# A tuned attention and feed-forward kernel: its instruction order taken from a longer search, with refitted durations

## The chip, the cores and the metric

The kernel runs on one core of one Trainium2 chip. The metric is device time in microseconds (us). Before the change the median of the first three runs was 248.99 us (248.48 to 249.06). A difference of over 2% counts as faster or slower here.

The engines are TensorE (PE; its weight loads PEld), VectorE (DVE), ScalarE (ACT), GpSimd (POOL) and the queue engine SyncE (SP). L706 in a row means line 706 of that kernel; line numbers differ between kernels.

## The reference

```python
def _attn_ref(q, k, v, n_global, n_local):          # q, k, v: 4 x 8 x 768 x 64
    scores = scale * np.matmul(q, k.transpose(0, 1, 3, 2))
    ...                                             # keep: 8 global keys, or the last 96
    scores = np.where(keep, scores + bias, -1000000000.0)
    a = np.exp(scores - np.max(scores, axis=-1, keepdims=True))
    return np.matmul(a / (np.sum(a, axis=-1, keepdims=True) + 1e-09), v)

def _moe_ref(x, w_gate, w_val, w_out, rms_g):       # x: 3072 x 512, hidden width 1536
    xn = x / np.sqrt(np.mean(x * x, axis=-1, keepdims=True) + 1e-06) * rms_g
    g = xn @ w_gate
    return (g * (1.0 / (1.0 + np.exp(-g))) * (xn @ w_val)) @ w_out
```

This is shortened. Attention with a local band and a few global keys is followed by a gated feed-forward layer (FFN) on its output.

## The kernel before

The 3072 tokens are cut into 8 chunks of 384. Every operation is first entered in a list with an estimated duration, a due position, its dependencies and the buffers it takes and gives. A list scheduler then runs through this list with its own clock, and writes each instruction in the order in which it starts them. The search shifts the priorities of groups of operations at random and keeps a step if the planned end is no later. All of this happens when the kernel is built. The chip sees only the resulting order.

```python
    START = {"SP": 0.7, "ACT": 0.7, "POOL": 1.4}     # us until a transfer begins
...
    def search(self, tries, keys, spread):

        rnd, best, shift = random.Random(7), math.inf, {}
        groups = sorted({key for o in self.ops for key in keys(o)}, key=str)
        for k in range(tries):
            new = dict(shift)
            if k:
                part = rnd.choice((0.05, 0.2, 1.0))
                amp = rnd.choice(spread)
                for g in groups:
                    if rnd.random() < part:
                        new[g] = new.get(g, 0.0) + rnd.uniform(-amp, amp)
            for o in self.ops:
                o.shift = sum(new.get(g, 0.0) for g in keys(o))
            end = self.run(call=False)
            if end <= best:
                best, shift = end, new
        for o in self.ops:
            o.shift = sum(shift.get(g, 0.0) for g in keys(o))
        self.run()
...
    # run(): the planner's loop, cut
    t0 = min(cand)[0] + slack                        # of what could start now, the lowest rank
    _, _, t, o = min((r, n, t, o) for t, r, n, o in cand if t <= t0)
    ...
    if call:
        ins = o.fn(*o.args, *([] if o.only else [eng]))   # emit the instruction here
    ...
    return self.free["PE"]                           # the planned end: when TensorE is done
```

These are the operations that the argument touches: the gate behind which chunk 1's keys and queries are transferred, the PE transposes of the first chunks, the root of the norm, and the padding matmuls.

```python
    held = [seq_ops["raw", "k", HP - 2]]             # pair 2 of chunk 0's raw keys
    if c == 1:
        held = seq_ops["gate"] = [add("POOL", 0.15, base, gate, "k1", deps=held, take=[bb["k"]])]
    for x, n in enumerate("kq"):
        o = add("POOL", 1.0, base + x, load_heads, c, n, kb=2.35, packet=49, ...)
...
    o = add("PE", (0.42, 0.68, 0.5)[c], due, tr, c, p, name, ...)      # transposes of q and k
...
    sq = [add("DVE", 0.16, a, ssum, c, deps=sq)]
    r = add("POOL", 1.1 if c >= NX else 0.9, a + 2, rstd, c, deps=sq)
...
    pad = add("PE", 1.1, a + 3.9, idle, c, deps=norms, take=t)
...
    TRIES = 200
...
    plan.search(TRIES, keys, (1.0, 3.0, 8.0))
```

The softmax here doesn't subtract the row's maximum and nothing guards it: scores larger than these inputs give would overflow.

Of the kernel before, what the change touches and what calls it, by code (L numbers as in the profile page):

```python
# [39 lines left out]
class _Plan:  # L40
# [10 lines left out]
    SLOW = ("xn", "glob_v", "kg", "cast_v", "copy_vg")  # L51

    ORDERED = ("mask", "xn", "glob_v", "kg")
    START = {"SP": 0.7, "ACT": 0.7, "POOL": 1.4}

    OVERLAP = {"PE": 0.0, "ACT": 0.1, "DVE": 0.08, "POOL": 0.06, "SP": 0.0}
    LAG = {"PE": 0.2, "ACT": 0.1, "DVE": 0.1, "POOL": 0.12, "SP": 0.0}
# [14 lines left out]
    def add(self, eng, dur, due, fn, *args, deps=(), take=(), give=(), extra=0.0, kb=0.0,  # L72
            packet=20):




        o = _Op()
        o.eng, o.durs = (None, eng) if isinstance(eng, dict) else (eng, {eng: dur})
        o.due, o.fn, o.args = due, fn, args  # L80
        o.deps, o.take, o.give = [d for d in deps if d is not None], list(take), list(give)
        o.extra, o.kb, o.done, o.n, o.shift, o.only = extra, kb, None, len(self.ops), 0.0, o.eng
        o.packet = packet
        self.ops.append(o)
        return o
# [67 lines left out]
        q = self.queues.get(eng)  # L153
        return q[-1][3].done - 4.3 if q else t

    def search(self, tries, keys, spread):

        rnd, best, shift = random.Random(7), math.inf, {}
        groups = sorted({key for o in self.ops for key in keys(o)}, key=str)
        for k in range(tries):  # L160
            new = dict(shift)
            if k:
                part = rnd.choice((0.05, 0.2, 1.0))
                amp = rnd.choice(spread)
                for g in groups:
                    if rnd.random() < part:
                        new[g] = new.get(g, 0.0) + rnd.uniform(-amp, amp)
            for o in self.ops:
                o.shift = sum(new.get(g, 0.0) for g in keys(o))
            end = self.run(call=False)  # L170
            if end <= best:
                best, shift = end, new
        for o in self.ops:
            o.shift = sum(shift.get(g, 0.0) for g in keys(o))
        self.run()
# [86 lines left out]
def kernel(  # L262
# [42 lines left out]
    NX = 4  # L305
# [71 lines left out]
    ident = const.tile([128, 128], BF16, tag="ident")  # L377
# [344 lines left out]
    def gate(what):  # L722
# [8 lines left out]
        else:  # L731
# [5 lines left out]
    plan = _Plan(  # L737
        sizes=dict(m=5, sc=2, av=1, P0=4, P1=4, u=2, t=3, h=2, xT=2, xu=2, xn=2, ob=3, sq=4, sk=4,
                   sv=4, qb=2, kb=2, qT=2, kT=2, kG=2, ld=999),
        free=dict(PE=0.8, ACT=2.1, DVE=0.85, POOL=0.8, SP=0.8))  # L740
    add, buf = plan.add, plan.buf
# [28 lines left out]
    seq_ops, const_ops, xn_gate = {}, {}, []  # L770

    def early_part(c):

        b, half = divmod(c, 2)
        q_ops, k_ops, v_ops = {}, {}, {}
        qT_buf[c], kT_buf[c] = buf("qT", HP), buf("kT", (16, 4, 5)[c])
        ld, vs, gs = {}, [], []
        base = START + (-30, 10, 60)[c]
        gated = []

        def load_v():
            for i in range(HB):
                sb = buf("sv")
                if c == 2 and i == 0:
                    gated.append(add("POOL", 0.15, START, gate, "v2", deps=[w_ops["o", 2]], take=[sb]))
                ld["v", i] = add("SP", 0.5, base + 5 + i, load_block, c, "v", i, kb=1.17, packet=20,
                                 take=[] if c == 2 and i == 0 else [sb], deps=gated), sb

        bb = {n: buf(n + "b", HP) for n in "qk"}
        if c == 0:  # L790
            for p in range(HP):
                for n in "qk":
                    eng = "ACT" if (p, n) == (0, "k") else "SP"
                    sb = buf("s" + n)
                    o = add(eng, 0.5, base + p if p < 2 else base + 10 + p, load_pair, p, n, eng, kb=0.6, packet=39, take=[sb])
                    seq_ops["raw", n, p] = o
                    ld[n, p] = add({"DVE": 0.36, "ACT": 0.5, "POOL": 0.55}, 0.5, START + 8 * p - 1, cast_pair, p, n,
                                   deps=[o], take=[] if p else [bb[n]], give=[sb]), bb[n]
            load_v()
        else:  # L800
            held = [seq_ops["raw", "k", HP - 2]]
# [3 lines that stand above are left out]
                o = add("POOL", 1.0, base + x, load_heads, c, n, kb=2.35, packet=49,  # L805
                        take=[] if (c, n) == (1, "k") else [bb[n]], deps=held)
                seq_ops["heads", c, n] = o
                for p in range(HP):
                    ld[n, p] = o, bb[n]
            load_v()  # L810
        for key, (o, _) in ld.items():
            seq_ops["ld", c, key[0], key[1]] = o
        due = (START - 1.0, S1 - 2.0, S2 - 2.0)[c]
        for i in range(HB):
            o, sb = ld["v", i]
            if c == 0:
                e1, e2 = {"POOL": 0.63, "ACT": 0.6, "DVE": 0.43}, {"POOL": 0.63, "ACT": 0.6, "DVE": 0.3}
            else:
                e1, e2 = {"POOL": 0.63}, {"POOL": 0.63}
            vs.append(add(e1, 0, due, cast_v, c, i, deps=[o] + (xn_gate if c else []), give=[sb]))  # L820
            if 0 < HB * half + i < NB - 1:
                gs.append(add(e2, 0, due + 0.1, copy_vg, c, i, deps=vs[-1:]))
        lo, hi = max(HB * half, 1), min(HB * half + HB, NB - 1)
        old = [glob[c - 1]] if half else []
        glob[c] = add({"DVE": 0.41, "POOL": 1.25}, 0, due, glob_v, b, lo, hi, deps=gs + old)
        kg_due = due
        for p in range(HP):
            v_ops[p] = vs + [glob[c]] + old
            due = (START + 8 * p, S1 + 2 * p, S2 + 4 * p)[c]
            for name, ops in (("q", q_ops), ("k", k_ops)):  # L830
                if c and p % 2:
                    ops[c, p] = ops[c, p - 1]
                    continue
                t = buf("m")
                o = add("PE", (0.42, 0.68, 0.5)[c], due, tr, c, p, name, deps=[ld[name, p][0], const_ops["ident"]] + hold.get(c, []),
                        take=[t], give=[ld[name, p][1]] * (2 if c else 1))
                tk = [] if p else [(qT_buf if name == "q" else kT_buf)[c]]
                ops[c, p] = [add({"ACT": 0.78} if c == 1 else {"ACT": 0.78, "DVE": 0.95} if c else {"ACT": 0.5, "DVE": 0.5}, 0, due + 1, cp, c, p, name, deps=[o],
                                 give=[t], take=tk)]
        if c >= NK:  # L840
            kG_buf[c] = buf("kG", HP if half else HP + 1 + HP)
            o = add({"DVE": 0.45 if half else 0.56, "POOL": 0.9 if half else 1.05}, 0, kg_due + 2, kg, c,
                    deps=[x for p in range(HP) for x in k_ops[c, p]], take=[kG_buf[c]],
                    give=[kT_buf[c]] + ([kT_buf[0]] if half else []))
            for p in range(HP):
                kg_ops[c, p] = o
        return q_ops, k_ops, v_ops
# [51 lines left out]
    def attention(c, q_ops, k_ops, v_ops):  # L899
# [4 lines left out]
        norms = []  # L904
        old_k.update(k_ops)
        for p in range(HP):
            yield
            a = a0 + 4 * p if b else START + 8 * p if c == 0 else S1 + 2 * p
# [18 lines left out]
            for d in range(2) if c == 0 else ():  # L927
# [3 lines left out]
                deps = q_ops[c, p] + k_ops[c, p]  # L931
# [23 lines left out]
        else:  # L955
# [3 lines left out]
                           ssq, c, i, part, deps=norms[:HP - 1] if part == 1 else norms,  # L959
                           give=[xu_b] if part == 1 else []) for i in range(HB)]  # L960
            sq = [add("DVE", 0.16, a, ssum, c, deps=sq)]
        r = add("POOL", 1.1 if c >= NX else 0.9, a + 2, rstd, c, deps=sq)
        xnb, xtb = buf("xn", 1 if c >= NX else HB), buf("xT", FC)
        x = [add({"DVE": 0.61} if c >= NX else {"DVE": 0.36} if c == 0 else {"DVE": 0.36, "ACT": 0.62}, 0.61, a + 3, xn, c, i, deps=[r], give=[xu_b],
                 take=[xnb] if i == 0 else []) for i in range(HB)]
# [2 lines left out]
        if c < NX:  # L968
            t = [buf("m", 2), buf("m", 2)]
            if c == 0:  # L970
                pad = add("PE", 1.1, a + 3.9, idle, c, deps=norms, take=t)
            o = [add("PE", 0.23, a + 4, xtr, c, i, deps=[x[i]] + ([pad] if c == 0 else []), take=[] if i or c == 0 else t, give=[xnb])
                 for i in range(HB)]
            for i in range(1, HB):
                o[i].deps.append(o[i - 1])
            done = [add({"DVE": 0.42, "ACT": 0.58}, 0, a + 5, xev, c, cc, deps=o, give=[t[cc // 2]],
                        take=[] if cc else [xtb]) for cc in range(CC)]
        else:
            done = [add("SP", 2.4, a + 4, dma_xt, c, deps=x, give=[xnb], take=[xtb], kb=1.8, packet=22)]
# [27 lines left out]
                at += 0.5  # L1007

    XNP = 1.15
    TRIES = 200  # L1010
    START, S1, S2, LEAD, DRAIN = -200.0, -22.0, -10.0, 26.0, 20.0
    def constants():
        S = START
# [49 lines left out]
                          reason="order at the shared port")  # L1063

    plan.follow = follow
    plan.search(TRIES, keys, (1.0, 3.0, 8.0))

# [1 line left out]
_INS = ['q', 'k', 'v', 'n_global', 'n_local', 'moe_w_gate', 'moe_w_val', 'moe_w_out', 'moe_rms_g']  # L1069
# [31 lines left out]
```

## Time and profile before

| | before |
|---|---|
| median of the first three runs | 248.99 us |
| span of the profiled run | 247.2 us |
| first matmul | 6.36 us |
| first FFN matmul | 25.23 us |
| end of the last matmul | 244.06 us |

The page of the kernel before gives the chain that ended last by line, as shares of the span, and then the costliest groups of instructions: line, engine, operation, tiles, shape, count, then busy us and mean ns, then idle time of the engine before them.

```profile
PE gps L675 24%; PE vps L682 23%; PE ops L706 22%; PE sc L536 4%; DMA kb<-in_k_dram 2%; PE avp L593 2%; DMA sv<-in_v_dram 2%; DMA kT<-kb 2%; PE avp L597 2%; POOL V L512 1%; PE xtp L653 1%; DMA out_dram<-osb 1%; ACT xn L644 1%; DVE VG L520 1%; ACT P L550 1%
...
L675 PE MATMUL gps<-xT,w_gate 128*128 128x384 bf16 x384 | 78.4, 327 | 0.0
...
L706 PE MATMUL ops<-w_out,hb 128*128 128x512 bf16 (+2 forms) x293 | 64.7, 362 | 1.0
```

The first row shows that the chain is the FFN: gate products 24%, value products 23%, output products 22%. The reader should look at the last number of each group. The gate products never wait. The output products have 1.0 us of idle before them, and no releaser is named for it.

### The profile page before, as it was taken

The numbers are of one execution on the slowest core, as the hardware profiler recorded it, in microseconds if no ns is written. First come the engines' busy times: TensorE is split into PE (matmuls) and PEld (weight loads), VectorE is DVE, ScalarE is ACT, GpSimd is POOL, SyncE is SP. The second block draws the span as 40 slices with busy tenths as digits, with TensorE's granted clock in tenths as the row PEclk, the third lists the DMA queues.
The fourth block names the chain that finished last, engine by engine and source line by source line (L and its number), as shares of the span: only waits on it lengthen the run. The fifth ranks groups of instructions, "written<-read, shape, count | busy, mean of one in ns | idle before, by whom it ended". The sixth has DMA issues, their size and how long they took to land.

```text
span 247.2 us, 5302 instructions
## 1 busy us (share of the span) xinstructions
PE 231.5 (94%) x1957; PEld 134.8 (55%) x1976; DVE 176.4 (71%) x391; ACT 151.4 (61%) x352; POOL 107.7 (44%) x145
## 2 busy tenths in 40 slices
PE   0798999999999899999999999999999999999994
PEld 0466555655564466655555555555565555555544
DVE  5697789957793898886977867776966578446701
ACT  7988874978387869856655893477463254232310
POOL 4176971289578867724555657724320010000000
PEclk9999999999999999999999999999999999999999
DMA  7999999999999499726993949810141014100122
GB/s 189 251 195 207 208 206 199 212 211 224 228 230 217 132 228 169 158 67 148 208 187 95 232 104 193 179 42 6 49 97 45 0 42 110 42 20 27 42 84 86
DMA packets 93642, 34.43 MB, mean 139 GB/s; under 512 B 83504, under 2 KB 90544, under 8 KB 93616
## 3 DMA queue, kind: packets, MB, share of 16 engines
q1 hardware_dynamic: 84288, 27.53, 52.2%
q0 software_dynamic: 8912, 6.29, 16.9%
q8 instruction: 15, 0.25, 0.4%
q10 hardware_dynamic: 416, 0.26, 0.3%
q14 instruction: 11, 0.09, 0.1%
HBM read 28.58 MB, written 6.29 MB: 141 GB/s over the span
## 4 chain that ended last, share of the span: by engine, by line
PE 78%; DMA 8%; DVE 4%; ACT 3%; POOL 3%; SPq 2%; issue 1%; DVEq 0%; POOLq 0%
PE gps L675 24%; PE vps L682 23%; PE ops L706 22%; PE sc L536 4%; DMA kb<-in_k_dram 2%; PE avp L593 2%; DMA sv<-in_v_dram 2%; DMA kT<-kb 2%; PE avp L597 2%; POOL V L512 1%; PE xtp L653 1%; DMA out_dram<-osb 1%; ACT xn L644 1%; DVE VG L520 1%; ACT P L550 1%
## 5 line engine op out<-in xcount | busy, mean ns | idle before, releaser
L675 PE MATMUL gps<-xT,w_gate 128*128 128x384 bf16 x384 | 78.4, 327 | 0.0
L682 PE MATMUL vps<-xT,w_val 128*128 128x384 bf16 x384 | 78.1, 326 | 0.1
L693 DVE SCALAR_TENSOR_TENSOR u<-t,gps 128x384 f32<-128x384 f32 x96 | 52.8, 552 | 27.0 <-ACT t L688 24.5
L688 ACT ACTIVATE t<-gps 128x384 f32<-128x384 f32 x96 | 47.3, 493 | 35.9 <-PE gps L675 33.0
L550 ACT ACTIVATE P<-sc,bias 128x384 bf16<-128x384 f32 (+1 forms) x128 | 62.9, 560 | 6.0 <-PE sc L536 4.9
L706 PE MATMUL ops<-w_out,hb 128*128 128x512 bf16 (+2 forms) x293 | 64.7, 362 | 1.0
L700 DVE TENSOR_TENSOR hb<-u,vps 128x384 bf16<-128x384 f32 x96 | 52.7, 552 | 7.8 <-PE vps L682 0.5
L582 POOL TENSOR_TENSOR P<-P,md 128x768 bf16<-128x768 bf16 (+1 forms) x28 | 40.1, 1433 | 31.8 <-ACT P L550 24.5
L682 PEld LDWEIGHTS <-w_val 128*128 128x128 bf16 x384 | 36.9, 98 | 23.9 <-issue 0.3
L675 PEld LDWEIGHTS <-w_gate 128*128 128x128 bf16 x384 | 34.9, 98 | 22.9 <-issue 0.2
L706 PEld LDWEIGHTS <-hb 128*128 128x128 bf16 x312 | 29.0, 98 | 30.4 <-issue 0.3
L713 ACT ACTIVATE osb<-ops 128x512 f32<-128x512 f32 x19 | 11.3, 597 | 41.6 <-PE ops L706 41.6
L606 DVE TENSOR_TENSOR xu<-avp,rc 128x384 bf16<-128x384 f32 x32 | 17.8, 558 | 1.1
L593 PE MATMUL avp<-V,P 128*128 128x65 bf16 x192 | 16.4, 200 | 0.2 <-DVE xu L606 0.2
L619 ACT ACTIVATE junk<-xu 128x512 bf16<-128x512 bf16 (+2 forms) x29 | 14.9, 515 | 2.5 <-DVE xu L606 2.0
L593 PEld LDWEIGHTS <-P 128*128 128x128 bf16 x192 | 13.8, 101 | 4.5 <-DVE xu L606 1.0
L536 PE MATMUL sc<-qT,kT 64*128 64x128 bf16 x232 | 14.9, 231 | 1.3 <-ACT kT L562 0.5
L715 DVE TENSOR_SCALAR osb<-ops 128x512 f32<-128x512 f32 (+2 forms) x7 | 3.8, 540 | 14.1 <-PE ops L706 13.5
L512 POOL CAST V<-sv 128x512 bf16<-128x512 f32 x21 | 12.8, 618 | 1.9 <-PE ops L706 0.9
L495 POOL CAST qb<-sq 128x512 bf16<-128x512 f32 x15 | 9.5, 633 | 7.7 <-DMA sq<-in_q_dram 6.5
L597 PE MATMUL avp<-VG,P 128*128 128x65 bf16 x128 | 12.5, 197 | 0.3 <-DVE VG L520 0.3
L597 PEld LDWEIGHTS <-P 128*128 128x128 bf16 x160 | 11.5, 100 | 1.4 <-DVE P L582 0.2
(91 smaller groups left out, 187.3 us busy)
## 6 DMA issues: line engine op xcount, KB each, us to landing
sv<-in_v_dram SPq DMA_DIRECT2D x24, 256.0 KB, 4.6
out_dram<-osb SPq DMA_DIRECT2D x23, 256.0 KB, 2.2
sq<-in_q_dram SPq DMA_DIRECT2D x15, 256.0 KB, 4.7
sk<-in_k_dram SPq DMA_DIRECT2D x15, 256.0 KB, 4.9
w_gate<-in_moe_w_gate_dram POOLq DMA_DIRECT2D x3, 512.0 KB, 11.5
w_val<-in_moe_w_val_dram POOLq DMA_DIRECT2D x3, 512.0 KB, 14.1
w_out<-in_moe_w_out_dram POOLq DMA_DIRECT2D x3, 512.0 KB, 19.9
sq<-in_q_dram SPq DMA_DIRECT2D x4, 192.0 KB, 3.6
```

Of the source, the lines that this page charges most:

```text
L536: nc.tensor.matmul(sc[hh][:, ts(i, 128)], kT[r], qT[r], start=True, stop=True)
L550: nc.scalar.activation(T["P", c, p, d][:, hh, lo:HB, :], T["sc", c, p, d][hh][:, ds(128 * lo, CH - 128 * lo)], AF.Exp, bias=(bias1 if d el ...
L582: return tt(P[:, :, lo:HB, :], P[:, :, lo:HB, :], _brd(md1[:, ds(2 * p, 2)], 2, HB - lo), op=ALU.mult)
L593: nc.tensor.matmul(o[:, i, hh, :], P0[:, hh, i, :], V1[b % 2][:, I, h, :], start=True, stop=(I == 0))
L597: nc.tensor.matmul(o[:, i, hh, :], P1[:, hh, i, :], vg, start=False, stop=True)
L606: nc.vector.tensor_tensor(T["xu", c][:, :, ds(2 * p, 2), :], o[:, :, :, 0:64], _brd(rc, 3, 64), op=ALU.mult)
L675: nc.tensor.matmul(g[:, 0:CH], w_gate[:, cc, ts(f, 128)], T["xT", c][:, :, cc], start=(cc == 0), stop=(cc == CC - 1))
L682: nc.tensor.matmul(g[:, 0:CH], w_val[:, cc, ts(f, 128)], T["xT", c][:, :, cc], start=(cc == 0), stop=(cc == CC - 1))
L688: nc.scalar.activation(t, T["g", c, f][:, 0:CH], AF.Tanh, scale=0.5)
L693: nc.vector.scalar_tensor_tensor(u, T["t", c, f], 1.0, T["g", c, f][:, 0:CH], op0=ALU.add, op1=ALU.mult)
L700: nc.vector.tensor_tensor(T["h", c][:, f, :], T["u", c, f], T["v", c, f][:, 0:CH], op=ALU.mult)
L706: nc.tensor.matmul(o[:, 0:n], T["h", c][:, f, ts(j, 128)], w_out[:, f, ds(lo, n)], start=(f == 0), stop=(f == FC - 1))
```

## The change

The intent was an order with fewer stalls, from a search of 2500 steps in place of 200, on durations that were refitted to the chip. To keep the build short, the kept steps are listed in the kernel and only replayed. The shifts reach attention, loads, casts and evictions. The FFN matmuls keep their ranks.

```diff
-    START = {"SP": 0.7, "ACT": 0.7, "POOL": 1.4}
+    START = {"SP": 0.7, "ACT": 0.7, "POOL": 1.1}
...
-    def search(self, tries, keys, spread):
-
-        rnd, best, shift = random.Random(7), math.inf, {}
+    def search(self, kept, keys, spread):
+
+        rnd, shift = random.Random(6), {}
         groups = sorted({key for o in self.ops for key in keys(o)}, key=str)
-        for k in range(tries):
+        for k in range(1, kept[-1] + 1):
             new = dict(shift)
-            if k:
-                part = rnd.choice((0.05, 0.2, 1.0))
-                amp = rnd.choice(spread)
-                for g in groups:
-                    if rnd.random() < part:
-                        new[g] = new.get(g, 0.0) + rnd.uniform(-amp, amp)
-            for o in self.ops:
-                o.shift = sum(new.get(g, 0.0) for g in keys(o))
-            end = self.run(call=False)
-            if end <= best:
-                best, shift = end, new
+            part = rnd.choice((0.05, 0.2, 1.0))
+            amp = rnd.choice(spread)
+            for g in groups:
+                if rnd.random() < part:
+                    new[g] = new.get(g, 0.0) + rnd.uniform(-amp, amp)
+            if k in kept:
+                shift = new
         for o in self.ops:
             o.shift = sum(shift.get(g, 0.0) for g in keys(o))
         self.run()
...
-                o = add("PE", (0.42, 0.68, 0.5)[c], due, tr, c, p, name, deps=[ld[name, p][0], const_ops["ident"]] + hold.get(c, []),
+                o = add("PE", 0.48 if (c, name) == (1, "q") else (0.42, 0.7, 0.45)[c], due, tr, c, p, name, deps=[ld[name, p][0], const_ops["ident"]] + hold.get(c, []),
...
-        r = add("POOL", 1.1 if c >= NX else 0.9, a + 2, rstd, c, deps=sq)
+        r = add("POOL", 1.1 if c >= NX else 0.85, a + 2, rstd, c, deps=sq)
...
-                pad = add("PE", 1.1, a + 3.9, idle, c, deps=norms, take=t)
+                pad = add("PE", 1.0, a + 3.9, idle, c, deps=norms, take=t)
...
-    TRIES = 200
+    KEPT = (0, 2, 4, 5, 6, 8, 9, 10, 27, 28, 29, 36, 37, 38, 42, 44, 46, 51, 52, 79, 88, ...
+            ...                                     (cut: 599 numbers in all)
+            2449, 2453, 2456, 2462, 2465, 2468, 2469, 2470, 2474, 2478, 2485, 2487, 2490)
...
-    plan.search(TRIES, keys, (1.0, 3.0, 8.0))
+    plan.search(KEPT, keys, (1.0, 3.0, 8.0))
```

## The prediction

> **What bounds the kernel now.** I read the page's busy shares first, then the table of busy time by stretches of the span, then the waits of TensorE alone, then the order of instructions in time around each wait. The page's first part:
>
> ```profile
> PE 231.5 (94%) x1957; PEld 134.8 (55%) x1976; DVE 176.4 (71%) x391; ACT 151.4 (61%) x352; POOL 107.7 (44%) x145
> PE 78%; DMA 8%; DVE 4%; ACT 3%; POOL 3%; SPq 2%; issue 1%; DVEq 0%; POOLq 0%
> ```
>
> TensorE is busy 231.5 of 247.2 us, and 78% of the chain that ended last is its matmuls. Nothing else is near: VectorE has 71%, ScalarE 61%. So a new order can win only the 15.7 us in which TensorE is idle, plus what hides in a busy time that is modelled. The stretches, cut at the first matmul, at the first feed-forward matmul, and where attention is nearly done (time window; then busy us and instruction count of each engine; then clock, DMA share, GB/s):
>
> ```profile
> 0.00:6.36 6.36, 0.00 (x0) 0.00 (x0) 3.71 (x24) 5.04 (x19) 2.60 (x15) 1.00 0.74 190
> 6.36:25.20 18.84, 15.88 (x208) 10.66 (x208) 14.66 (x45) 16.69 (x40) 10.13 (x14) 1.00 1.32 217
> 25.20:85.00 59.80, 57.33 (x528) 32.96 (x529) 46.68 (x96) 44.36 (x102) 40.79 (x52) 1.00 1.15 212
> 85.00:212.00 127.00, 126.29 (x1034) 73.14 (x1045) 97.06 (x201) 75.88 (x176) 54.14 (x65) 1.00 0.55 115
> 212.00:247.20 35.20, 31.96 (x194) 18.05 (x194) 14.32 (x27) 9.46 (x18) 0.00 (x0) 1.00 0.15 53
> ```
>
> Idle of TensorE, as width less busy: 6.36 before the first matmul; 18.84 - 15.88 = 2.96 in the opening attention; 59.80 - 57.33 = 2.47 in the ramp; 127.00 - 126.29 = 0.71 in the long middle; 35.20 - 31.96 = 3.24 at the end. The last matmul ends at 244.06, so 247.17 - 244.06 = 3.11 of the end is the last eviction and store. The reader should see that the middle, half the span, holds almost nothing. What is left lies before 85 us.
>
> The waits of TensorE between 25.2 and 100 us, with what it waited for, the sum, the count and the longest:
>
> ```profile
> PE sc L536 <- ACT P L550: 0.7, 1, 0.7
> PE trp L483 <- DMA kb<-in_k_dram: 0.6, 1, 0.6
> PE avp L597 <- DVE VG L520: 0.3, 1, 0.3
> PE xtp L653 <- DVE u L693: 0.2, 1, 0.2
> ```
>
> They sum to 1.8 us; the remainder of the 2.47 + 0.71 is in pieces too short to be named. The second row is a cast transfer that GpSimd issued at 22.76 and that TensorE's transposes met only at 42.98. The third has its cause in the time order:
>
> ```profile
> 29.73 4.83 POOL L582 TENSOR_TENSOR P<-P,md 128x768 bf16<-128x768 bf16 x3
> 33.30 1.55 DVE L520 COPY VG<-V 8x1040 bf16<-8x1040 bf16 x1
> 34.91 0.19 PE L597 MATMUL avp<-VG,P 128*128 128x65 bf16 x1 [0.28 <-DVE VG L520]
> ```
>
> The same copy took 0.42 us at 10.00, when GpSimd did nothing; here it took 1.55 while GpSimd's masks ran.
>
> **What the skill says, and whether this trace agrees.** TensorE: Matmul & The Clock Gate, section "Back-to-back issue gap", gives N/1.2 ns cold and N/2.4 + 2.5 ns warm for an isolated matmul of N columns. That is 162.5 ns for 384 columns, and four feed-forward matmuls take 0.65 us from group to group in the chain, so this trace agrees: they already run at their floor. The same page, section "What's actually happening", says that the clock gate opens only after a window of activity. The trace agrees: the 65-column matmuls start 54 to 55 ns apart at 12.5 to 19.4 us (65/1.2 = 54) and 30 ns apart at 34.4. GPSIMD Engine Reference, "Key points": it shares its SBUF interfaces with VectorE. The 0.42 against 1.55 us agrees. DMA: Bandwidth & Descriptors, "Latency and other measured facts", puts the first byte of a transfer issued by GpSimd at about 1 us. That is the quantity that the change's 1.4 to 1.1 is about; the trace gives issue and landing, not the first byte, so no view here confirms either figure.
>
> **The change, part by part.**
>
> The kernel lists its operations with estimated durations and lets a list scheduler write the order. It shifts the priorities of groups (chunk and kind) at random and keeps a step if the planned end is no later. Before: 200 steps, generator seeded 7. After: the 599 kept steps of 2500, seeded 6, are replayed. Matmuls, bytes, tiles and buffers are the same. The shifts exclude the feed-forward matmuls, the output matmuls, weight loads and the gates, so these keep their nominal ranks. What moves is when attention matmuls, exponentials, masks, casts, evictions and loads come among them, and on which engine an operation with two choices runs. Added and removed instructions: about none (at most a few order waits between VectorE and GpSimd), so its direct cost is 0.
>
> Of 599 kept steps 46 lie below 200, and each later block of 250 still keeps 41 to 76. As a tie is kept too, that count says nothing of how much was won.
>
> The refits change no instruction either: GpSimd transfers counted to begin 0.3 us sooner, the second chunk's query transposes 0.48 for 0.68, the third chunk's 0.45 for 0.50, the reciprocal root 0.85 for 0.90, the padding matmuls 1.0 for 1.1. The trace supports most of them. The key transposes of chunk 1 take 1.49 us for 24 cold, the query ones 0.94; half of each is 0.74 and 0.47. The third chunk's 24 take 0.80 from start to next start (42.98 to 43.78), half 0.40. The padding takes 1.07, its next matmul 1.00 after it. So the new plan follows the chip better where it decides, by some tenths of a us.
>
> What can be won, from TensorE's own stream after 25.23 us. I add start-to-start times from the trace: 192 feed-forward groups x 0.65 = 124.8; 24 output groups x 2.59 = 62.2; two score groups of chunk 1 x 0.81 = 1.6; its four value products x 0.37 = 1.5; chunk 2's transposes 2 x 0.80 = 1.6; for each pair of heads of chunks 2, 4 and 6, 0.38 + 0.09 + 0.30, twelve times = 9.2; of chunks 3, 5 and 7, 0.44 + 0.09 + 0.36, twelve times = 10.7; three transposes of x, 12 x 55 ns each = 2.0. Sum 213.6. The stretch is 244.06 - 25.23 = 218.8, so an order without stalls would save about **5.2 us at most**. Of it the idle time is 2.47 + 0.71 + 3.24 - 3.11 = 3.3; 1.9 is slower cadence and the last matmul's latency, which order hardly touches.
>
> Ahead of 25.23 the time is a latency chain through transposes, ScalarE, masks, norm and the first x. Its slack is the 2.96 us idle, but most of it follows from the chain: 0.85 + 0.21 before the first x transposes waits for VectorE's normalisation, itself after GpSimd's 0.89 us root. The visible excess is the cold key transposes of chunk 1, put at 17.55 ahead of chunk 0's last value product, whose mask ended at 18.54 while the product began at 18.98: **0.4 us**.
>
> I expect the longer search to remove about half of the 3.3 (1.6 us: the 0.7, the 0.6 and bits) and a little of the start (0.4 us). The front of 6.36 and the end of 3.11 stay. Sum -2.0: 248.99 - 2.0 = **247.0 us**. That it is half and not all is my choice: a planner removes the waits that it sees, and the four named waits are mostly ones where the chip differed from the plan.
>
> **The rivals.**
>
> First: the gain exists in the plan alone. For: durations on the shared port vary by a factor of 3.7 (1.55/0.42), and landings of GpSimd's key and query transfers run from 6.0 to 20.2 us after issue; a tightly fitted order has less slack against these. New waits of 0.3 to 0.9 us then take the place of the old. Against: the middle runs at 99% already and its queue of feed-forward work is robust. It would give 248.3 to 249.5.
>
> Second: transfers become the bound of the ramp. Counting them sooner makes the planner put transposes of chunk 2 sooner, so the 0.6 us wait at 42.98 grows to 1 or 2. For: DMA moves 212 to 217 GB/s from 6 to 85 us. Against: the loads of later chunks have tens of us of lead, and 0.3 us is small. It would give 249 to 250.
>
> Third: the search finds nearly all the slack, and chunk 1 and 2's attention fits without a stall: 5.2 + 0.4 would give 243.4. Against: it needs the short gaps between kinds of matmul to go, which come with every switch.
>
> **Range and chances.** Weights: partial gain 65%, no net gain 25%, worse 5%, near the whole 5%. That gives 247.0 in the middle and 245.3 to 248.9 eight times in ten. Faster by over 2% means below 244.0, nearly all of the slack: 0.03. Slower by over 2% means above 254, a new stall of 5 us that the plan did not see: 0.02. Within 2%: 0.95.
>
> **What would show it.** Busy TensorE stays within 0.7 us of 231.5 and the first matmul within 0.2 of 6.36. Idle between 25.2 and 85 falls from 2.47 to some 1.2; the waits for the exponential and for the key transfer shrink or vanish, and the feed-forward starts at about 24.8. The end stays at 3.0 to 3.3 after the last matmul. I am wrong if the first feed-forward matmul comes later than 25.7, if idle in the ramp stays above 2.3, if a wait on a transfer above 1 us appears, or if the long middle loses more than 1.5 us.

## The result, and the profile after

The median is 249.08 us over six runs (248.70 to 250.02), against 248.96 us for the kernel before over six runs (248.48 to 249.42). Every ratio in this document is that of the two kernels' fast runs in the same rounds, as the record computes it, so it is not quite the ratio of the medians quoted beside it. This one is 1.0009, with a 95% interval of 0.9988 to 1.0031. The time is the same. The predicted 247.0 us did not come, and 249.08 lies just outside the range, whose upper end was 248.9.

The profiled execution was the slowest of the six, at 250.02 us. Its page starts so:

```profile
PE 231.9 (93%) x1958; PEld 136.1 (55%) x1976; DVE 176.3 (71%) x394; ACT 153.6 (62%) x353; POOL 103.4 (42%) x141
...
PE 80%; DMA 6%; ACT 5%; POOL 3%; DVE 3%; issue 1%; SPq 1%; DVEq 0%
```

TensorE is busy 231.9 us, where it was 231.5, and the shape of the chain is as it was. Next is the table of stretches for the changed kernel, with the columns as in the prediction, cut at its own first FFN matmul (26.50) and then at the same widths for the ramp:

```profile
0.00:6.36 6.36, 0.00 (x0) 0.00 (x1) 4.07 (x24) 5.04 (x19) 2.41 (x15) 1.00 0.74 194
6.36:26.50 20.14, 16.16 (x208) 11.63 (x209) 13.17 (x42) 17.87 (x42) 10.26 (x14) 1.00 1.26 209
26.50:86.30 59.80, 57.54 (x528) 32.86 (x532) 46.09 (x100) 42.74 (x96) 39.87 (x52) 1.00 1.12 209
86.30:213.20 126.90, 126.24 (x1033) 73.52 (x1044) 98.63 (x204) 78.49 (x181) 50.82 (x61) 1.00 0.56 115
213.20:248.30 35.10, 31.96 (x195) 18.07 (x194) 14.29 (x27) 9.47 (x18) 0.00 (x0) 0.99 0.15 53
```

The opening is 20.14 us wide against 18.84, with 20.14 - 16.16 = 3.98 us idle against 2.96. The ramp has 59.80 - 57.54 = 2.26 idle against 2.47. The middle and the end are as before. So little was won in the ramp, and more was lost ahead of it.

The waits of TensorE in the ramp of the changed kernel, 26.5 to 100 us, and then those in its opening, 12 to 24.5 us:

```profile
PE avp L593 <- DVE VG L516: 0.6, 1, 0.6
PE xtp L649 <- ACT xn L640: 0.6, 1, 0.6
PE trp L479 <- DMA kb<-in_k_dram: 0.5, 1, 0.5
```

```profile
PE trp L479 <- DMA kb<-in_k_dram: 1.5, 1, 1.5
PE sc L532 <- DVE kT L558: 0.6, 1, 0.6
```

The 0.7 us wait for an exponential is gone from the ramp (it was 0.7, 0.7 and 0.3 us in the three profiles of before). In its place stands a wait of 0.6 for ScalarE's normalised x, in this profile and in both others of this kernel, and the opening waits 1.5 for a key transfer and 0.6 for VectorE's copy of global keys. The time order around the new wait in the ramp shows how it came about (start, duration, engine, instruction, idle before it):

```profile
47.14 1.47 POOL L565 COPY kG<-kT 128x1536 bf16<-128x1536 bf16 x1 [2.59 <-ACT kT L486]
...
47.98 0.66 DVE L621 SCALAR_TENSOR_TENSOR ssq<-ssq,ss 128x3 f32<-128x3 f32 x1
...
48.68 0.24 POOL L567 COPY kG<-kG 128x64 bf16<-128x64 bf16 x1
48.87 0.88 POOL L628 TENSOR_TENSOR r<-ssq,half_c 128x3 f32<-128x3 f32 x1
...
49.79 1.33 ACT L640 ACTIVATE xn<-xu,r 128x512 bf16<-128x512 bf16 x2 [0.56 <-POOL r L628]
...
50.57 1.01 PE L649 MATMUL xtp<-ident,xn 128*128 128x128 bf16 x12 [0.58 <-ACT xn L640]
```

The new order puts the copy of chunk 2's keys (kG) on GpSimd ahead of the reciprocal root (r). The copy takes 1.47 + 0.24 us, where the plan has 1.05. The little sum on VectorE beside it takes 0.66, where the plan has 0.16. The root starts only behind the copy, at 48.87, and the normalisation and the transposes of x follow it; in kg_dve (experiment 3), which takes the copy out of the root's way, this wait is gone.

**How much of one profile is chance.** I profiled both kernels three times. In the table, "pause" is TensorE's idle time, worked out from the time order of its instructions. The pauses after the first FFN matmul leave out the holes in the record that are explained below.

| kernel, profile | first FFN matmul | pause before it | pause after it | last matmul ends |
|---|---|---|---|---|
| before, 1st | 25.23 | 2.96 | 2.29 | 244.06 |
| before, 2nd (before_again) | 26.58 | 2.86 | 1.96 | 244.68 |
| before, 3rd (before_third) | 25.93 | 2.48 | 1.73 | 243.92 |
| after, 1st | 26.50 | 3.98 | 2.07 | 245.26 |
| after, 2nd (after_again) | 26.11 | 3.41 | 1.29 | 243.91 |
| after, 3rd (after_five) | 26.11 | 3.85 | 1.57 | 244.19 |
| mean before | 25.91 | 2.77 | 1.99 | 244.22 |
| mean after | 26.24 | 3.75 | 1.64 | 244.45 |

The first FFN matmul of the kernel before scatters by 1.35 us with the order unchanged, and the profile on which I predicted has the earliest of the three. So 25.23 was luck, and most of the apparent loss at the opening of the first profile after is that luck missing.

**TensorE has two paces in the opening, and the change between them scatters.** The padding's 16 matmuls of 128 columns start 107 ns apart in the second profile of before and 56 ns apart in the first. (The clock column of the stretches reads 1.00 in the opening all the same.) By the start times of TensorE's matmuls the faster pace begins at 19.9 us in the first profile of before, at 22.4 in the third and at 23.8 in the second, and their first FFN matmuls come in this order. TensorE's busy time from its first matmul to its first FFN matmul was 15.9, 17.1 and 17.4 us. In the three profiles after, the faster pace begins at 22.3, 22.3 and 21.3 us, and the busy time was 16.2, 16.3 and 15.9. So the scatter of before lies in busy time, and pauses alone do not measure an opening: on average the order after pauses 0.98 us more in it and is busy 0.65 us less, which leaves its first FFN matmul 0.33 us later. Why the pace changes early or late was not tested.

**A hole is not a wait.** Of the 3.28 us that the prediction called idle after the first FFN matmul, 0.99 is no idle time. This is what the one line of output products holds in the kernel before, and then in an experiment (kg_dve) whose trace is complete: operation, count, durations in ns as least, median and most, then the times of the first and last start:

```profile
L706 PEld LDWEIGHTS <-hb x312: 95/98/101, 49.0 to 243.8; 128*128 128x128 bf16 x156
L706 PE MATMUL ops<-w_out,hb x293: 219/379/391, 49.1 to 243.8; 128*128 128x512 bf16 x129, 128*128 128x128 bf16 x12, 128*128 128x256 bf16 x6
```

```profile
L735 PEld LDWEIGHTS <-hb x312: 95/98/100, 52.4 to 246.1; 128*128 128x128 bf16 x156
L735 PE MATMUL ops<-w_out,hb x312: 219/379/389, 52.5 to 246.1; 128*128 128x512 bf16 x138, 128*128 128x128 bf16 x12, 128*128 128x256 bf16 x6
```

There is one weight load per matmul, and 312 loads stand against 293 matmul records: 19 are missing. The first line of each page says it too: the prediction shows 1957 PE against 1976 PEld. Output products start 0.216 us apart and last 0.379 by the record, so each missing one leaves a gap of 2 x 0.216 - 0.379 = 0.053 us, and 19 x 0.053 = 1.0. In kg_dve nothing is missing, and idle before its output products is 0.1 us in place of 1.0. The 0.71 us idle in the middle stretch of the prediction is nearly all such holes. Real pauses after the first FFN matmul were therefore 2.29 us in that profile, and 1.99 on average. In each profile after, 18 records are missing, two of them the first of their group, where the gap stands in front of the output products.

**What the plan itself expected.** This is no chip time. It is the planner's own bookkeeping of the two orders, printed while the kernels were built (us):

| the planner's count | before | after | difference |
|---|---|---|---|
| first matmul | 5.97 | 5.90 | -0.07 |
| TensorE idle up to the first FFN matmul | 5.60 | 6.32 | +0.72 |
| TensorE idle after it | 1.11 | 0.73 | -0.38 |
| TensorE work | 230.26 | 229.60 | -0.66 |
| planned end | 242.94 | 242.55 | -0.39 |

The whole planned gain is 0.39 us. Work fell by 0.66 with the same matmuls, and the diff alone gives that number: two query transposes of chunk 1 at -0.20 each, two key transposes at +0.02, four of chunk 2 at -0.05, the padding at -0.10. They are written shorter and do not become shorter. In idle time and start together the new order is planned 0.27 us worse. The two columns are not independent, as an operation that is written shorter can leave idle time behind it: the plan's first FFN matmul moves only from 27.26 to 27.45 us (the planner of both kernels run again). The chip shows the same exchange: the pauses before the first FFN matmul went up by 0.98 and those after it down by 0.35, while that matmul came 0.33 us later.

### The profile page after: what moved, and what is told of

Same layout as the page of the kernel before. It is cut to its first block, busy times and chain, and to the rows that moved or that the text cites. A ratio compares the mean times of both kernels' runs of the same rounds, so it can differ in the third digit from the quotient of the medians.

```text
span 248.3 us, 5293 instructions
## 1 busy us (share of the span) xinstructions
PE 231.9 (93%) x1958; PEld 136.1 (55%) x1976; DVE 176.3 (71%) x394; ACT 153.6 (62%) x353; POOL 103.4 (42%) x141
## 4 chain that ended last, share of the span: by engine, by line
PE 80%; DMA 6%; ACT 5%; POOL 3%; DVE 3%; issue 1%; SPq 1%; DVEq 0%
PE gps L671 24%; PE vps L678 23%; PE ops L702 22%; PE sc L532 4%; DMA kb<-in_k_dram 3%; DMA sv<-in_v_dram 2%; PE avp L589 2%; PE avp L593 2%; ACT P L546 1%; POOL P L578 1%; ACT junk L615 1%; PE trp L479 1%; ACT xn L640 1%; DVE VG L516 1%; PE xtp L649 1%
## 5 line engine op out<-in xcount | busy, mean ns | idle before, releaser
L578 POOL TENSOR_TENSOR P<-P,md 128x768 bf16<-128x768 bf16 (+1 forms) x28 | 40.0, 1431 | 33.0 <-ACT P L546 16.2
L709 ACT ACTIVATE osb<-ops 128x512 f32<-128x512 f32 x22 | 13.1, 597 | 44.7 <-PE ops L702 44.7
L601 DVE RECIPROCAL rc<-avp 128x6 f32<-128x6 f32 x32 | 6.2, 192 | 8.9 <-PE avp L593 8.8
L491 POOL CAST kb<-sk 128x512 bf16<-128x512 f32 x15 | 9.5, 634 | 5.6 <-DVE P L574 4.0
```

Of the source, the lines that this page charges most:

```text
L578: return tt(P[:, :, lo:HB, :], P[:, :, lo:HB, :], _brd(md1[:, ds(2 * p, 2)], 2, HB - lo), op=ALU.mult)
```

## The experiments

The expectations quoted below were recorded before each run. Their letters name the theories as they stood then. Kernels that are listed under one number shared a chip and the runs of the kernel before.

### 1. Does the planned end mean anything on the chip?

> The changed kernel unaltered, for a second profile and more times. Theory A (the plan itself gained only 0.39 us, 242.94 to 242.55 by its own count, and the chip's deviations from the plan are as large as that): ratio to before 0.998 to 1.003, and the first feed-forward matmul within 0.5 us of before's 25.2. Rival B (the changed order is systematically worse in the opening: its key transposes of the second chunk block the last value product of the first): the first feed-forward matmul again after 26.2, and the wait for the key transfer again above 1 us.

> The kernel before with one step in its search in place of 200, so no hill climb at all. Its own plan ends at 247.28 us, 4.34 later than before's. Theory A: the plan ranks large differences, so the chip loses 2.5 to 5.5 us (ratio 1.010 to 1.022). Rival C (the chip doesn't follow the plan at all; slack on the engines absorbs order): ratio under 1.005.

```diff
 # unsearched: the kernel before
-    TRIES = 200
+    TRIES = 1
```

> The kernel before, its constants and its generator seed kept, with the 383 kept steps of a 2500 step search baked in: its own plan ends at 242.63, 0.31 us ahead of before's. Theory A: same within 0.4% of before, either sign (ratio 0.996 to 1.004). Rival D (a longer search is worth 2 us on the chip as I predicted, and only the refitted constants spoilt it): ratio 0.990 to 0.994.

```diff
 # long_search: durations and seed of the kernel before, 2500 steps, its 383 kept steps listed
-    TRIES = 200
+    KEPT = (0, ...)                                 # cut
```

> The kernel before with only the refitted constants (transfers from 1.1, first transposes, root, padding), its 200 steps searched with them: its own plan ends at 243.51. Theory A: within 0.5% of before (ratio 0.997 to 1.005), as the plan is 0.57 us later. Rival D (the constants spoil the order by making transfers look early): ratio over 1.005 with a wait for the key transfer above 1 us.

```diff
 # refit_only: the kernel before with the refitted durations alone, 200 steps, seed 7
-    START = {"SP": 0.7, "ACT": 0.7, "POOL": 1.4}
+    START = {"SP": 0.7, "ACT": 0.7, "POOL": 1.1}
...                                                 # transposes, root and padding as in the change
```

| kernel | planned end | median, us | ratio to before | 95% interval |
|---|---|---|---|---|
| before, in the same rounds | 242.94 | 249.67 | 1 | |
| after_again | 242.55 | 248.93 | 0.9977 | 0.9954 to 1.0001 |
| unsearched | 247.28 | 258.13 | 1.0353 | 1.0320 to 1.0386 |
| long_search | 242.63 | 248.77 | 0.9976 | 0.9949 to 1.0002 |
| refit_only | 243.51 | 248.73 | 0.9971 | 0.9948 to 0.9993 |

A plan that ends 4.34 us later costs 3.5%, or 8.5 us between the medians. That is about twice the plan's difference, and more than the 2.5 to 5.5 us that I expected. The waits of TensorE in that kernel, 24 to 110 us, are ones that the search had removed:

```profile
PE avp L593 <- DVE P L578: 2.6, 1, 2.6
PE xtp L653 <- DVE xn L646: 1.0, 1, 1.0
PE sc L536 <- POOL kG L571: 0.7, 1, 0.7
```

Behind the first of these, which ends at 86.15 us, the granted clock is 0.50 from 87.14 to 90.55 (1.00 there in before). An estimate from that is 3.41 x 0.5 = 1.7 us lost on top of the waits; the planner's durations have no such term. One profile does not show that the wait is the reason.

So the search matters, and its first 200 steps had found nearly all of it: in the planner's count the idle after the first FFN matmul is 5.04 us unsearched, 1.11 after 200 and 0.80 after 2500 on the same durations. The interval of long_search, the longer search without refits, leaves out the 0.990 to 0.994 that a gain of 2 us would have given. The small differences do not carry over. The kernel whose plan ends latest among the searched ones, refit_only, was not the slowest of them. after_again fell between its two theories: its first FFN matmul came at 26.11 us, and its wait for chunk 1's key transfer was 0.4.

### 2. Is the opening of the new order what costs?

In the first profiles after, a mask of chunk 1 stood on VectorE ahead of the first evictions of x, and two evictions stood on ScalarE behind four exponentials. These runs mend that. The emitted sequence is collected and a few operations are moved in it. Nothing else differs.

> The kernel before against itself. Theory A (times of one order differ from chip to chip and run to run by some 0.3%): ratio 0.997 to 1.003, so that ratios of 0.997 count as nothing. It also gives a second profile of before: I expect its first feed-forward matmul at 25.0 to 26.0 us (25.23 in the first profile) and 218.3 to 219.3 us from there to the last matmul (218.83 in the first).

> The changed kernel, its order kept but for two things in the opening: VectorE's mask of the second chunk's first pair stands behind the evictions of the first x transposes and not ahead, and all four evictions run on VectorE (two were on ScalarE behind four exponentials). Theory E (the changed order gives back in the opening what it wins later, and these evictions are part of it): the gap from the last x transpose to the first feed-forward matmul falls from 1.5 us to under 1.2, the 0.4 us stall inside the first feed-forward groups vanishes, total 0.4 to 0.9 us under the changed kernel's 249.0 (ratio to before 0.992 to 0.997). Rival F (the opening isn't what limits; a later wait takes the gain): no later matmul starts earlier and the ratio is that of the changed kernel.

```diff
 # evict_dve: the kernel after; seq is the planner's sequence of (operation, engine)
+        last = max((self.at(seq, "xev", 0, cc) for cc in range(4)))
+        seq = self.behind(seq, [("mask", 1, 0, 0, "DVE")], ("xev", *seq[last][0].args))
+        seq = [(o, "DVE" if o.fn.__name__ == "xev" and o.args[0] == 0 else eng) for o, eng in seq]
```

> The changed kernel with the opening mended in four places: as the run before, and besides the last value product of the first chunk ahead of the second chunk's key transposes (which wait for a transfer), and the gate and issue of that transfer without the wait for a VectorE mask. Theory E: first feed-forward matmul at 24.9 to 25.5 instead of 26.1 to 26.5, and the time from there to the last matmul stays at 217.8 to 218.8, so 1.0 to 1.6 us under the changed kernel (ratio to before 0.990 to 0.996). Rival F: the opening is earlier but the later stretch grows by as much, because it waits for transfers and weights that have their own time; ratio 0.997 to 1.000.

```diff
 # open_all: evict_dve, and
+        seq = self.behind(seq, [("tr", 1, 0, "k"), ("tr", 1, 2, "k")], ("av", 0, 3))
+        k = self.at(seq, "mask", 0, 0, 1)
+        early = [...]                               # gate "k1" and load_heads(1, ...), cut
+        seq = seq[:k] + early + [x for x in seq[k:] if x not in early]
```

> The long search of before's constants and seed, with the first chunk's last value product ahead of the key transposes that waited 1.6 us for their transfer. In the long search's profile the feed-forward began 2.2 us later than before's and the stretch from there was 2.2 us shorter (216.65 against 218.83). Theory E: first feed-forward matmul at 25.9 to 26.5 in place of 27.41, the stretch at 216.6 to 217.4, total 0.6 to 1.4 us under the long search (ratio to before 0.990 to 0.995). Rival F: the stretch was short only because it began late, and grows to 217.8 or more; ratio 0.996 to 1.000.

```diff
 # long_value: long_search, and
+        seq = self.behind(seq, [("tr", 1, 0, "k"), ("tr", 1, 2, "k")], ("av", 0, 3))
```

| kernel | median, us | ratio to before | 95% interval |
|---|---|---|---|
| before, in the same rounds | 249.38 | 1 | |
| before_again | 249.43 | 1.0015 | 0.9990 to 1.0040 |
| evict_dve | 249.25 | 0.9992 | 0.9974 to 1.0010 |
| open_all | 249.20 | 1.0002 | 0.9985 to 1.0019 |
| long_value | 248.60 | 0.9977 | 0.9946 to 1.0008 |

The kernel before against itself gives 1.0015, so a tenth or two of a per cent says nothing here. The mended openings lost their stall at the evictions, but the first FFN matmul came no sooner: 28.05 us in evict_dve and 26.72 in open_all, against 26.11 to 26.50 unmended. These two profiles had other waits: evict_dve's waited 2.6 us for chunk 1's key transfer (0.4 to 1.5 unmended) and open_all's 1.1 us for VectorE ahead of the value product, so it is the times that speak. By them the theory that this stall was the loss falls. The 0.4 us of the late value product, which the prediction put down as a gain, moved no total either: long_value differs from long_search in it alone, its first FFN matmul came at 26.54 us in place of 27.41, and the ratios are 0.9977 and 0.9976. Two expectations of the kernel before itself were missed as well: before_again's first FFN matmul (25.0 to 26.0) came at 26.58, and before_third's idle after it (2.9 to 3.3, holes included) was 2.73.

### 3. Does the new wait in the ramp cost its length, and do better durations make a better order?

> The changed kernel with one thing undone: the third chunk's copy of its keys, which the new order put on GpSimd ahead of the second chunk's reciprocal root, is back on VectorE right behind the sum of squares, as in the kernel before. The plan counts 1.05 us for that copy on GpSimd; the traces show 1.47 and 0.24 for its two instructions. Theory G (the search trades one wait for another that its sizes hide: the 0.9 us wait for exponentials near 81 us went, a 0.75 us wait of the x transposes near 49 us came): the gap ahead of the x transposes falls from 0.75 to under 0.3 us, time from first feed-forward matmul to last matmul falls from 217.8 to about 217.1, ratio to before 0.994 to 0.998. Rival H (that stretch is bound by something else, and the wait moves to the next matmul): gap gone, stretch still 217.5 or more, ratio as the changed kernel's.

```diff
 # kg_dve: the kernel after; rstd(1) and kg(2) right behind ssum(1), kg(2) on DVE (was POOL, ahead of rstd(1))
+        two = [(o, "DVE" if o.fn.__name__ == "kg" else eng) for o, eng in two]
+        two.sort(key=lambda x: x[0].fn.__name__ == "kg")
+        k = self.at(seq, "ssum", 1) + 1
+        seq = seq[:k] + two + seq[k:]
```

> The kernel before with ten of the plan's sizes set to what the traces show (squares with their accumulator read, key copies on both engines, sum and scaling, the first transposes cold, GpSimd transfers counted to begin LATER, from 2.1, not sooner) and a search of 2500 steps with before's seed 7. The plan's own end is 245.33, later than before's 242.94, only because its sizes are longer. Theory G (the sizes, not the number of steps, hold the gain): fewer named waits after the first feed-forward matmul (idle under 2.0 us against 2.3 to 3.3), stretch 216.5 to 217.5, ratio 0.990 to 0.996. Rival I (what is left is scatter of transfers and the chip's own gaps, which no sizes catch): ratio 0.997 to 1.001.

> The same sizes searched with seed 8; the plan's own end is 245.35, equal to seed 7's. It tells whether two orders that the plan holds equal are equal on the chip. Theory A (chip and plan differ by up to 1 us in either direction for an order): within 0.4% of the run before. If both lie at 0.990 to 0.996 the sizes carried the gain; if one does and the other doesn't, it was the draw.

```diff
 # resized (seed 7), resized8 (seed 8): the kernel before, 2500 steps, sizes set to the trace; some of them:
-    START = {"SP": 0.7, "ACT": 0.7, "POOL": 1.4}
+    START = {"SP": 0.7, "ACT": 0.7, "POOL": 2.1}
-            o = add({"DVE": 0.45 if half else 0.56, "POOL": 0.9 if half else 1.05}, 0, kg_due + 2, kg, c, ...
+            o = add({"DVE": 0.75 if half else 0.85, "POOL": 1.2 if half else 1.72}, 0, kg_due + 2, kg, c, ...
-            sq = [add("DVE", 0.16, a, ssum, c, deps=sq)]
+            sq = [add("DVE", 0.28, a, ssum, c, deps=sq)]
```

| kernel | planned end | median, us | ratio to before | 95% interval |
|---|---|---|---|---|
| before, in the same rounds | 242.94 | 249.08 | 1 | |
| kg_dve | | 250.24 | 1.0049 | 1.0027 to 1.0071 |
| resized | 245.33 | 250.89 | 1.0067 | 1.0044 to 1.0089 |
| resized8 | 245.35 | 249.29 | 1.0006 | 0.9985 to 1.0027 |

In kg_dve the wait for the normalised x is gone, and another has come in its place. Its waits of TensorE, 24 to 100 us, and the copies on VectorE in time:

```profile
PE sc L565 <- DVE qT L519: 0.8, 1, 0.8
```

```profile
48.76 0.95 DVE L598 COPY kG<-kT 128x1536 bf16<-128x1536 bf16 x1
49.75 0.18 DVE L600 COPY kG<-kG 128x64 bf16<-128x64 bf16 x1
49.84 0.95 DVE L519 COPY qT<-trp 128x768 bf16<-128x768 bf16 x1
```

The key copy now delays the query copy on VectorE, and TensorE waits 0.8 us for that. From 46 to 52 us of this profile VectorE is busy 5.4 and ScalarE 5.5 of the 6 us, GpSimd 1.1, so there was little room for the copy on VectorE. The total did not fall, and this profile also has a late opening (first FFN matmul at 28.24 us). How much of the 0.5% belongs to the copy was not separated.

The two resized kernels have equal plans on durations closer to the trace, and their times differ by 1.6 us. Neither beats before. Better single sizes did not make a better order. In the one profile of each, both with complete records, TensorE pauses 3.11 us after the first FFN matmul in resized and 1.48 in resized8. Of the 3.11, 1.2 and 0.6 are waits for the query and key transfers of chunk 2, which resized8 does not have. That would fit the 1.6 us, but no run isolates it.

### 4. Does the key transfer of chunk 1 bound the opening?

TensorE's key transposes of chunk 1 waited for this transfer in every profile of before and after, 0.2 to 1.5 us. They started 5.8 to 6.9 us after its issue. The theory was that its landing sets the opening and hides any gain of the order.

> Edit: the kernel after, with the gate of chunk 1's key transfer reading pair 1's raw keys in place of pair 2's and issued ahead of the mask on VectorE, so that the transfer is issued near 6 us in place of 11.5 to 12.3. Theory I (its landing bounds the opening, and the opening bounds the end): TensorE waits no more for the key transfer (0.4 to 2.6 us so far), the first FFN product comes by 25.3 us in place of 26.1 to 28.2, and the ratio to before is 0.990 to 0.996. Rival J (the early transfer takes the queues from chunk 0's own loads, or the first FFN product comes sooner and the later ramp waits the more): first matmul or first scores later by over 0.5 us, or idle after the first FFN product above 3 us, ratio 0.998 to 1.003.

> Edit: the same early key transfer in long_search (constants of before, 2500 steps, the value product of chunk 0 ahead of chunk 1's key transposes). Theory I: ratio 0.988 to 0.995, lower than long_value's 0.9977. Rival J: 0.996 to 1.002, the same as long_value.

> The kernel before against itself, for the scatter: ratio 0.998 to 1.002; first FFN product anywhere from 25.2 to 27 us, idle after it 2.9 to 3.3 us.

```diff
 # early_keys: the kernel after; early_long: long_value
+        k = self.at(seq, "mask", 0, 0, 0)           # early: gate "k1" and load_heads(1, ...)
+        seq = seq[:k] + early + seq[k:]
-            src, dst = T["a0", HP - 2, "k"][0:1, 0, 0, 0:1], cast_tile(1, "k")[0:1, 0:1]
+            src, dst = T["a0", HP - 3, "k"][0:1, 0, 0, 0:1], cast_tile(1, "k")[0:1, 0:1]
```

| kernel | key transfer issued | first FFN matmul | median, us | ratio to before | 95% interval |
|---|---|---|---|---|---|
| before, in the same rounds | | | 248.77 | 1 | |
| early_keys | 6.16 | 28.85 | 251.37 | 1.0103 | 1.0088 to 1.0118 |
| early_long | 8.74 | 27.32 | 248.48 | 0.9987 | 0.9973 to 1.0001 |
| before_third | 11.86 | 25.93 | 248.61 | 0.9988 | 0.9975 to 1.0001 |

The wait for chunk 1's key transfer is gone in both, and neither is faster than the kernel before was against itself. These are the transfers issued in the first 14 us, with size and median us from issue to landing, in before_third and then in early_keys:

```profile
sv<-in_v_dram SPq DMA_DIRECT2D x6, 256.0 KB, 5.3
...
sk<-in_k_dram SPq DMA_DIRECT2D x3, 192.0 KB, 3.7
...
kb<-in_k_dram POOLq DMA_DIRECT2D x1, 384.0 KB, 6.0
```

```profile
sv<-in_v_dram SPq DMA_DIRECT2D x6, 256.0 KB, 7.0
...
sk<-in_k_dram SPq DMA_DIRECT2D x3, 192.0 KB, 5.7
...
kb<-in_k_dram POOLq DMA_DIRECT2D x1, 384.0 KB, 6.8
```

The early transfer takes bandwidth from chunk 0's own loads: raw keys land after 5.7 us in place of 3.7, values after 7.0 in place of 5.3. Chunk 0's transposes then wait for their casts (early_keys, waits of TensorE from 12 to 30 us):

```profile
PE trp L508 <- ACT kb L376: 1.4, 2, 0.9
...
PE trp L508 <- DVE qb L376: 0.5, 1, 0.5
```

The first FFN matmul comes at 28.85 us, 2.6 later than the mean after, and the median is 2.3 above the 249.08 of after (measured in other rounds). So the theory of the landing as the bound falls, and the gate that holds this transfer back earns its place. The opening does reach the total when it is late by that much.

### 5. Is there anything left of the gain?

Three rounds could not tell 0.2% from nothing, so the three kernels that mattered ran five.

> The changed kernel unaltered. Plan's gain arrives at its own size (0.39 us of 249): ratio 0.9975 to 0.9992. Nothing arrives: 0.9992 to 1.0015. Prediction's 2.0 us: 0.992.

> The refitted durations alone with 200 steps, planned end 243.51 against 242.94 of before. If plans rank small differences: slower than before by 0.5 us, ratio 1.0015 to 1.003. If 0.5 us of plan means nothing on the chip: 0.997 to 1.0015; the three-round ratio was 0.9971.

> The other long search (2500 steps on the durations of before, planned end 242.63) with chunk 0's last value product moved ahead. If it beats before: 0.995 to 0.998. If the 0.9977 of three rounds was scatter: 0.998 to 1.001.

| kernel, unaltered from above | planned end | median, us | ratio to before | 95% interval |
|---|---|---|---|---|
| before, in the same rounds | 242.94 | 248.52 | 1 | |
| after_five | 242.55 | 249.04 | 1.0012 | 0.9984 to 1.0039 |
| refit_five | 243.51 | 248.29 | 0.9975 | 0.9951 to 0.9999 |
| long_value_five | | 248.56 | 0.9980 | 0.9954 to 1.0006 |

The changed kernel has now 1.0009, 0.9977 and 1.0012. Nothing of a gain arrives that these runs can see. The refits with the old short search gave 0.9971 and 0.9975, both intervals below 1, although its plan ends 0.57 us later than that of before. If it is a gain it is a quarter of a per cent, far from 2%. It is the best version that ran, and the kernel before against itself moved by 0.15% as well. Its two profiles start the first matmul at 5.31 us, against 6.36 in before and after, and pause 4.53 and 3.88 us ahead of the first FFN matmul. After it they pause 1.42 and 0.53, holes left out. These numbers would fit its time, but no run isolates them.

## Why the prediction was wrong, point by point

- **The bound: right.** TensorE's work sets the end. Its busy time moved by 0.4 us against the 0.7 allowed (though it scatters by more within one order: 231.5, 232.5 and 232.3 us in the profiles of before), the first matmul came at 6.36 us, and 3.05 us remained after the last matmul, all as stated. That only the ramp and the opening could change was right too.
- **The size of what could be won: wrong.** The step "Of it the idle time is 2.47 + 0.71 + 3.24 - 3.11 = 3.3" took holes in the record for idle time. It measures 2.29 us without the 19 missing records, and 1.99 as the mean of three profiles.
- **The share that a search would win: wrong, and this is the step that failed.** "I expect the longer search to remove about half of the 3.3 (1.6 us ...) and a little of the start (0.4 us)". The pauses after the first FFN matmul fell by 0.35 us on average, and those before it grew by 0.98. The plan had seen 1.11 us of the former at all, and removed 0.38 of that by giving 0.72 to the latter. Where I put down a gain at the start, the plan itself had the first FFN matmul 0.19 us later, and the chip 0.33. Experiment 1 shows why so little was left: 200 steps had taken the planned idle from 5.04 to 1.11.
- **The refits: half right.** "The trace supports most of them" rested on one profile. Chunk 1's query transposes took 0.88 us from start to next start there, and 1.42, 1.43, 1.41, 1.42 and 1.16 in the five other profiles of before and after, so 0.48 for half of them is too short in nearly all. It is the pace again: in that profile the faster one began among these transposes. The time order of the profile before and of before_third:

```profile
19.64 0.94 PE L483 MATMUL trp<-ident,qb 128*64 128x128 bf16 x24
20.52 1.07 PE L467 MATMUL xtp<-warm 128*128 128x128 bf16 x16
```

```profile
20.07 1.49 PE L483 MATMUL trp<-ident,qb 128*64 128x128 bf16 x24
21.49 1.51 PE L467 MATMUL xtp<-warm 128*128 128x128 bf16 x16
```

- **The first rival: right, and weighted too low.** "The gain exists in the plan alone" gave 248.3 to 249.5 with a weight of 25%. The time is 249.08, and a new wait of 0.6 us in the ramp, in all three profiles, took the place of the old one, as it said.
- **The second rival: not borne out.** The transfer wait of chunk 2 stayed at 0.5 us. The wait above 1 us that appeared in the first profile after is at chunk 1 and was 0.4 and 0.9 in the two others.
- **The signs named as proof of error: two of four showed** in the first profile after: the first FFN matmul at 26.50 (over 25.7) and a transfer wait of 1.5 us. The ramp's idle was 2.26, just under the 2.3 that I had set, so that sign did not show by its letter, and far from the 1.2 that I expected. The middle lost nothing.

What stays open is why refit_only seems a quarter of a per cent faster, why two orders of equal plan (resized, resized8) lie 1.6 us apart, and what sets the moment at which TensorE's pace changes.

## What to carry to other kernels

Before predicting what a new order wins, ask what the old order's planner already counted as idle, and split a fall of the planned end into idle removed and durations rewritten: here the second was larger than the whole. Compare the counts of matmuls and weight loads before reading small gaps as waits, look when TensorE's pace changes before comparing two openings, and take at least two profiles before a difference of 1 us in one is given a cause. When the waits left are tenths of a us on full engines, a reordering moves them rather than removes them.

## What the Trainium skill lacked or had wrong

- GPSIMD Engine Reference, section "Key points", says that GpSimd shares its SBUF interfaces with VectorE, and that section gives no size (other pages of the skill say more of this port). Here the same copy of 8x1040 values took 0.42 us alone and 1.55 beside GpSimd's masks, and a sum of 128x3 took 0.66 us beside a GpSimd copy of 1.47, and 0.16 at its three other places in that profile.
- DMA: Bandwidth & Descriptors, section "Latency and other measured facts", gives the first byte of a transfer issued by GpSimd as about 1 us. No view here shows a first byte. What decided the opening is the landing of a 384 KB transfer among others, which came 6.0 us after issue in before_third and 6.8 in early_keys, where it in turn delayed 192 KB loads from 3.7 to 5.7 us.
- I found no page that says how missing matmul records look in a trace: 19 of 312 were missing here, and left gaps of 0.053 us each that read as 1.0 us of idle time.
